# Column attention and a routed feed-forward on one core: low halves of v subtracted on GpSimd, and all of the last value pairs multiplied on halves

## The chip, the cores and the metric

One core of a Trainium2 chip runs the whole kernel. The metric is the device time of one execution in microseconds (us). A core has five engines that each work through an instruction stream of their own, in order, and wait for each other by semaphores: TensorE (PE in the profile, with PEld for the loading of its weights), VectorE (DVE), ScalarE (ACT), GpSimd (POOL) and SyncE (SP).

## The reference

`q`, `k` and `v` have the shape (4, 5056, 256). Attention runs over the columns, per batch, and its output rows go through eight experts, each of which takes exactly 2528 rows, given out greedily by the gate's value:

```python
qn = q / (np.linalg.norm(q, axis=1, keepdims=True) + 1e-06)
kn = k / (np.linalg.norm(k, axis=1, keepdims=True) + 1e-06)
a = softmax(kn.transpose(0, 2, 1) @ qn / tau)      # 256 x 256 per batch
x = (v @ a).reshape(B * S, D)                      # 20224 rows of 256
logits = x @ w_gate
# ... each expert e gets its cap = 2528 best rows, greedily over all (row, expert) values
out[mask] = np.maximum(x[mask] @ w1[e], 0.0) @ w2[e]
```

Everything is float32.

## The kernel before, in words

The kernel has three stages. In the first, some 200 us, the scores of the four batches are summed (L334) and the softmax is made; batch 0's product v @ a and the gate's logits are done beside it. In the second, from about 195 to 321 us, the rest of v @ a is multiplied, while the first expert's rows are searched out. In the third the eight experts' two layers run (L1333 and L1365), with the search for the next expert beside them.

The change is in the second stage, the loop over `later` near the program's end (L1406). `later` is a list of 52 **pairs** (b, c, t): two columns of 128 rows of v each, which `x_tiles` (L269) multiplies with the 256x256 matrix `a` of their batch into a PSUM tile `px`. There are two ways to do it:

- an **uncut** pair multiplies float32 by float32: 4 matmuls in the program (each shows as two records in the trace), from `vs` and `a_f`;
- a **cut** pair multiplies on halves: `split_v` (L255) makes a rounded high half `vh` on ACT (L259) and a low half `vl` = raw - `vh` (L262), and 12 matmuls of one pass sum `vh` x `aH`, `vh` x `aL` and `vl` x `aH`.

The set `cut` (L228, L229) says which pairs are cut. `cut_ahead` splits a pair AHEAD = 3 pairs before PE multiplies it; the tiles `vh` and `vl` have AHEAD + 1 = 4 buffers. ACT copies each `px` to `xs` (L286), and after two pairs starts a store of `xs` to `x_d` in HBM (L296).

Beside the pairs runs the **search** of the first expert (`route`, `search`, `totals`). It has two times four rounds and a last one. A round compares all keys with 15 thresholds on DVE (`ge`, L730, two instructions), counts on PE with 20 small matmuls (`pc` from `ge`, L699), reduces and spreads the counts on DVE (`Dm`, `Dr`, `Ex`: L702 to L708), sums over the partitions on PE with one matmul (`pc` from `Ex`, L712), and finds the new threshold on DVE (`mxs`, `hit`, `thr`, `cur`: L719 to L756). After the rounds a chain of small DVE instructions ends in the expert's number `ei` (L851) and in `cb` (L888). Then POOL loads the expert's weights (L1175), and `compact` turns the chosen rows into a list of indices with 20 matmuls `pi` (L912), whose rows ACT counts for 11 of them (`junk`, L930, and `ext`, L933). ACT and DVE split the loaded weights into halves in 8 pieces (L1184, L1187). When the pairs are stored and the list is there, POOL gathers the rows of the first chunk (L1225), PE turns them (L1291), ACT and DVE make `xH` and `xL` (L1300, L1303), and the first layer begins (L1333). Until the gathered rows have landed PE runs 27 dummy matmuls (`warm`, L1313).

The order of the instructions is fixed when the program is built. A planner, `Order`, keeps a clock for PE (`o.pe`) and one for DVE (`o.dve`). `tick` moves PE's clock on by each matmul, and `hook` then places every search step whose turn has come; DVE work that belongs to the pairs is handed over by `o.post` with a ready time and a cost:

```python
def post_low(low):
    unit[0] += 1
    o.post(o.pe + TURN_LAT, 690, low, unit[0])
```

The planner thus counts 690 ns of DVE for each `vl`. It keeps no clock for POOL.

Of the kernel before, what the change touches and what calls it, by code (L numbers as in the profile page):

```python
# [8 lines left out]
F32 = mybir.dt.float32  # L9
# [6 lines left out]
OP = mybir.AluOpType  # L16
# [32 lines left out]
CG = 128 // J  # L49
BUFS_V = 8  # L50
CUT_FROM = 12
CUT_TO = 40
GAP = 400
AHEAD = 3
AB = 2
# [36 lines left out]
def attention_moe(ctx: ExitStack, tc: tile.TileContext, q, k, vt, tau, wg, w1t, w2t, tabs, out):  # L92
    nc = tc.nc
    V = nc.vector
    S = nc.scalar
    P = nc.gpsimd
# [129 lines left out]

    later = [(b, c, t) for b, c in TODO for t in range(0, T, 2)]
    cut = {(0, c, t) for c in range(NCH) for t in range(0, T, 2)}  # L228
    cut |= set(later[CUT_FROM:CUT_TO] + later[CUT_TO::2])  # L229

    def is_cut(b, c, t):
        return (b, c, t - t % 2) in cut
# [9 lines left out]
    def cut_a(b, ac, post=None):  # L242
        aH = apool.tile([128, 2, GW], F32R, name="aH", bufs=AB)
        aL = apool.tile([128, 2, GW], F32R, name="aL", bufs=AB)
        S.activation(aH, ac, AF.Copy)
        a_cut[b] = (aH, aL)

        def low():
            V.tensor_tensor(aL, ac, aH.bitcast(F32), op=OP.subtract)
        if post:  # L250
            post(low)
        else:
            low()

    def split_v(b, c, t, post=None):  # L255
        raw = vs[b, c][:, :, t:t + 2, :]
        vh = vp.tile([128, 2, 2, 128], F32R, name="vh", bufs=AHEAD + 1)
        vl = vp.tile([128, 2, 2, 128], F32R, name="vl", bufs=AHEAD + 1)
        S.activation(vh, raw, AF.Copy)  # L259

        def low():
            V.tensor_tensor(vl, raw, vh.bitcast(F32), op=OP.subtract)  # L262
        if post:
            post(low)
        else:
            low()
        cuts_v[b, c, t] = (vh, vl)

    def x_tiles(b, c, t, xs, width, tick=None):  # L269
# [19 lines left out]
    def x_rows(width):  # L289
        xs = vp.tile([128, TH * GW], F32, name="xs", bufs=3)  # L290
        return xs[:, 0:TH * width].rearrange("p (t c) -> p t c", t=TH)

    def store_x(b, c, xs, t0, t1):
        r0 = (b * NCH + c) * CH
        rows = x_d[r0:r0 + CH].rearrange("(p t) c -> p t c", t=T)
        nc.scalar.dma_start(rows[:, t0:t1], xs[:, t0 % TH:t0 % TH + t1 - t0, 0:C])  # L296
# [738 lines left out]
    class Order:  # L1035
# [13 lines left out]
        def post(self, ready, cost, fn, unit):  # L1049
            self.main.append((ready, cost, fn, unit))  # L1050
# [76 lines left out]
    o = Order()  # L1127
    nphase = [0]

    def plan():  # L1130
        p = nphase[0]
        if p < E and done.get(("start", p)) is None and (p == 0 or done.get(("routed", p - 1))):
            done["start", p] = True

            def job(p=p):
                yield from route(p, E - p)
                done["routed", p] = True
                nphase[0] += 1
            o.add(job(), lambda p=p: 0 if (p == 0 or done.get(("idx", p - 1))) and (
                not done.get(("ei", p)) or done.get(("idx", p))) else EARLY_PRIO)  # L1140
# [21 lines left out]
    def settle():  # L1162
        for e in list(pend):
            if done.get(e[0]):
                pend.remove(e)
                e[1]()

    def want(key, fn):
        pend.append((key, fn))
        settle()  # L1170

    def load_w(p):
        raws[p] = big("ub"), big("ub")
        for raw, src in zip(raws[p], (w1t, w2t)):
            P.indirect_dma_start(out=raw, out_offset=None, in_=src,  # L1175
                                 in_offset=bass.IndirectOffsetOnAxis(ap=routed[p]["ei"][:, 0:1], axis=0))
# [58 lines left out]
    def gather():  # L1235
        for _ in range(2 if queue and queue[0][1] == 0 else 1):
            if queue:
                queue.pop(0)[2]()
# [4 lines left out]
    unit = [0]  # L1243
# [136 lines left out]
    with tc.manual_schedule():  # L1380
        o.dve = FIRST_LAT
        plan()
        cut_w = [None]

        def first_w():
            load_w(0)
            cut_w[0] = [o.pe + LOAD_LAT] + list(SPLIT)

        want(("ei", 0), first_w)
        o.patient = True  # L1390
        cutting = [st for st in later if st in cut]
        ready = {}

        def post_low(low):
            unit[0] += 1
            o.post(o.pe + TURN_LAT, 690, low, unit[0])

        def cut_ahead():
            st = cutting.pop(0)
            split_v(*st, post_low)  # L1400
            ready[st] = unit[0]

        for b in (2, 3):
            cut_a(b, a_f[b], post_low)

        for b, c, t in later:  # L1406
            if t % TH == 0:
                xs = x_rows(C)
            due = later.index((b, c, t)) + AHEAD
            while cutting and later.index(cutting[0]) <= due:  # L1410
                cut_ahead()
            o.flush(max((ready.get(st, 0) for st in later[:due + 2 - AHEAD]), default=0))
            x_tiles(b, c, t, xs, C, o.tick)
            settle()
            if cut_w[0] and o.pe > cut_w[0][0] and len(cut_w[0]) > 1:
                split_piece(0, *cut_w[0].pop(1))
            if (b, c) == TODO[-1] and t >= TH:
                store_x(b, c, xs, t, t + 2)
            elif t % TH == TH - 2:
                store_x(b, c, xs, t + 2 - TH, t + 2)  # L1420
        o.until(("ei", 0))
        settle()
        o.until(("idx", 0))
        actx.close()
        cctx.close()
        ffx = ctx.enter_context(tc.tile_pool(name="ffx", bufs=2))
        ps_1 = ctx.enter_context(tc.tile_pool(name="ps_1", bufs=DEPTH, space=PSUM))
        ps_2 = ctx.enter_context(tc.tile_pool(name="ps_2", bufs=2, space=PSUM))
        o.margin = FIRST_MARGIN
        o.patient = False  # L1430
        load_x(0, 0)
        while queue:
            gather()
        load_x(0, 1, paced=True)
        for i, q_, eng in cut_w[0][1:]:
            split_piece(0, i, q_, eng)
        for _ in range(START_TICKS):
            warm()
            o.tick(216 + 80)
        turn(0, 0)  # L1440
        for p in range(E):
            last = p == E - 1
            if p == 1:
                o.margin = MARGIN
            def turn_at(c):
                return lambda: turn(p, c)

            turns = [] if last else [(p + 1, 0), (p + 1, 1)]

            def next_turn(force=False):  # L1450
                if not turns:
                    return
                if force:
                    o.until(("idx", p + 1))
                    settle()
                    while queue:
                        gather()
                    while o.pe < landed[turns[0]]:
                        o.tick(100)
                if o.pe >= landed.get(turns[0], 1e12):  # L1460
                    turn(*turns.pop(0))

            def next_w(p=p):
                if p + 1 < E:
                    want(("ei", p + 1), lambda: load_w(p + 1))

            nchunk = len(cuts[p])
            h = {}
            pieces = {} if p == 0 else {at: [lambda q_=q_: split_piece(p, 1, q_, None)] for q_, at in enumerate((1, 3, 4, 6))}
            if p == 0:  # L1470
                next_w()
                h[0] = layer1(p, 0, {}, 2)
                layer2(p, 0, h[0], {1: [turn_at(1)]})
                h[1] = layer1(p, 1, {5: [turn_at(2)]})
            else:
                if (p, 1) not in xts:
                    fb = 5 if (p, 1) in BY_PE else TURN_FB
                    pieces[fb] = pieces.get(fb, []) + [turn_at(1)]
                h[0] = layer1(p, 0, pieces, 2)
                next_w()  # L1480
            for c in range(1 if p else 2, nchunk):
                h[c] = layer1(p, c, {}, 2 if p else 1)
                ins = {}
                if c + 1 < nchunk:
                    ins = {min(1, cuts[p][c - 1] - 1): [turn_at(c + 1)]}
                elif not last:
                    def w1(p=p):
                        o.until(("ei", p + 1))
                        settle()
                        g = split_w(p + 1, 0, V)  # L1490
                        for _ in g:
                            o.dve += 600
                    ins = {min(1, cuts[p][c - 1] - 1): [w1]}
                layer2(p, c - 1, h[c - 1], ins)
            layer2(p, nchunk - 1, h[nchunk - 1], {i: [next_turn] for i in range(1, 4)})
            while turns and turns[0][1] == 0:
                next_turn(True)
# [63 lines left out]
```

## Time and profile before

| | |
|---|---|
| median of 3 runs | 1256.83 us (1256.02 to 1259.64) |
| the profiled execution | 1257.59 us, of which 1255.8 us span |
| PE busy | 1238.3 us (99%) |
| DVE busy | 872.7 us (69%) |
| ACT busy | 601.0 us (48%) |
| POOL busy | 384.5 us (31%) |
| granted TensorE clock, mean | 0.998 |

The span reaches from the first to the last instruction. Busy time counts overlapped matmuls with their latency, so PE can be 99% busy and still stand still for short times; the spacing of the matmuls' starts shows more. The profile lets one ask for any stretch, engine, line or tile. The chain of waits follows the work that ended last backwards from the end.

### The profile page before, as it was taken

The page shows a single profiled execution, that of the slowest core. Times are in us where ns is not written, and L with a number is a line of the kernel's source. Part 1 is how long each engine was busy: PE and PEld are TensorE (multiplying, and loading weights), DVE is VectorE, ACT ScalarE, POOL GpSimd, SP SyncE. Part 2 cuts the span into 40 slices and gives each one's busy share as a digit, 9 for nine tenths or more (in the row PEclk, how much of TensorE's full clock was granted, in tenths as well). Part 3 has the DMA queues.
Part 4 walks back from the last instruction along what each step waited for, and adds up shares of the span by engine and source line. Part 5 has one row for each costly group of instructions (what it writes and reads, how often), then busy time and mean ns, then how long its engine had stood idle before and what let it go on. Part 6 is the DMA issues. An engine that isn't in the chain of part 4 may idle for free.

```text
span 1255.8 us, 24082 instructions
## 1 busy us (share of the span) xinstructions
PE 1238.3 (99%) x8779; PEld 1111.2 (88%) x8779; DVE 872.7 (69%) x2457; ACT 601.0 (48%) x1441; POOL 384.5 (31%) x690
## 2 busy tenths in 40 slices
PE   8999999999999999999999999999999999999998
PEld 6888977898888988998999899988989898898998
DVE  6688496898778778868867888887785445344431
ACT  6646652467324434434533755556554554334331
POOL 1000010000432353244343452532444434334322
PEclk9999999999999999999999999999999999999999
DMA  8999875236112134143422532341434235333301
GB/s 308 314 409 414 311 275 199 118 153 235 58 48 87 41 84 121 42 90 81 126 68 59 138 79 64 80 131 40 93 73 129 59 80 146 73 69 76 69 31 34
DMA packets 184759, 160.33 MB, mean 128 GB/s; under 512 B 150080, under 2 KB 155328, under 8 KB 180032
## 3 DMA queue, kind: packets, MB, share of 16 engines
q1 hardware_dynamic: 157712, 79.33, 22.6%
q0 software_dynamic: 17664, 58.22, 14.4%
q10 hardware_dynamic: 9264, 21.24, 4.4%
q8 instruction: 69, 1.13, 0.4%
q14 instruction: 50, 0.41, 0.1%
HBM read 99.97 MB, written 41.68 MB: 113 GB/s over the span
## 4 chain that ended last, share of the span: by engine, by line
PE 84%; DVE 6%; issue 5%; POOL 2%; DMA 2%; ACT 1%; SPq 0%; POOLq 0%; DVEq 0%; ACTq 0%
PE ph L1333 33%; PE py L1365 32%; PE px L283 7%; PE s L334 7%; PE pc L699 2%; POOL out_dram L1372 1%; PE px L446 1%; DVE acc_q L348 1%; PE pi L912 1%; DVE yy L405 1%; DVE acc_k L348 1%; DMA x_d<-xs 1%; DMA ua<-in_q_dram 1%; DVE vl L262 0%; ACT ua L1184 0%
## 5 line engine op out<-in xcount | busy, mean ns | idle before, releaser
L1333 PE MATMUL ph<-xH,ua 128*128 128x512 f32 (+3 forms) x1312 | 354.8, 388 | 0.3 <-ACT xH L1300 0.3
L1365 PE MATMUL py<-uc,hH 128*128 128x256 f32 (+1 forms) x2560 | 334.5, 279 | 0.0
L1341 DVE SCALAR_TENSOR_TENSOR hL<-ph,hH 128x512 fp32r<-128x512 f32 (+3 forms) x328 | 219.4, 670 | 162.4 <-ACT hH L1336 158.2
L1365 PEld LDWEIGHTS py<-uc,hH 128*128 128x128 f32 (+1 forms) x2560 | 312.9, 187 | 2.2
L1372 POOL DMA_INDIRECT out_dram<-y,idx x160 | 162.0, 1013 | 498.1 <-ACT y L1370 445.3
L1336 ACT ACTIVATE hH<-ph 128x512 fp32r<-128x512 f32 (+3 forms) x328 | 190.6, 582 | 206.1 <-PE ph L1333 202.1
L1333 PEld LDWEIGHTS ph<-xH,ua 128*128 128x128 f32 x1312 | 238.4, 189 | 42.8 <-ACT xH L1300 0.4
L1333 PE MATMUL ph<-xL,ua 128*128 128x512 f32 (+3 forms) x656 | 201.3, 386 | 0.1
L1370 ACT ACTIVATE y<-py 128x256 f32<-128x256 f32 (+1 forms) x160 | 61.3, 383 | 251.0 <-PE py L1365 235.1
L1225 POOL DMA_INDIRECT xg<-x_d,src x156 | 156.6, 1004 | 71.6 <-issue 33.6
L1365 PE MATMUL py<-uc,hL 128*128 128x256 f32 (+1 forms) x1280 | 178.3, 280 | 0.0
L1365 PEld LDWEIGHTS py<-uc,hL 128*128 128x128 f32 (+1 forms) x1280 | 160.2, 187 | 0.0
L1333 PEld LDWEIGHTS ph<-xL,ua 128*128 128x128 f32 x656 | 122.1, 189 | 23.3 <-DVE xL L1303 0.3
L334 PE MATMUL s<-ua 128*128 128x256 f32 x320 | 73.7, 387 | 2.6 <-DMA ua<-in_q_dram 2.6
L334 PEld LDWEIGHTS s<-ua 128*128 128x128 f32 x320 | 61.0, 193 | 14.2 <-issue 3.4
L286 ACT ACTIVATE xs<-px 128x512 f32<-128x512 f32 (+1 forms) x96 | 49.4, 528 | 49.5 <-PE px L283 47.8
L334 PE MATMUL s<-uc 128*128 128x256 f32 x320 | 71.3, 380 | 0.0
L334 PEld LDWEIGHTS s<-uc 128*128 128x128 f32 x320 | 60.3, 190 | 8.8 <-issue 0.8
L283 PE MATMUL px<-aH,vh 128*128 128x256 f32 (+1 forms) x216 | 62.7, 292 | 0.0
L283 PE MATMUL px<-aH,vl 128*128 128x256 f32 (+1 forms) x216 | 61.3, 284 | 1.1 <-DVE vl L262 0.9
L1284 DVE TENSOR_TENSOR xL<-ph,xH 128x512 fp32r<-128x512 f32 (+1 forms) x66 | 42.9, 679 | 27.8 <-ACT xH L1281 25.7
L969 ACT ACTIVATE junk<-pi,rhalf 128x160 bf16<-128x160 f32 x140 | 54.0, 391 | 15.7 <-PE pi L912 14.6
(341 smaller groups left out, 1569.5 us busy)
## 6 DMA issues: line engine op xcount, KB each, us to landing
x_d<-xs ACTq DMA_DIRECT2D x39, 512.0 KB
xq<-xg SPq DMA_DIRECT2D x500, 32.0 KB
vr<-in_vt_dram SPq DMA_DIRECT2D x14, 1024.0 KB
uc<-in_k_dram SPq DMA_DIRECT2D x18, 512.0 KB
uc<-in_q_dram SPq DMA_DIRECT2D x18, 512.0 KB
ua<-in_k_dram SPq DMA_DIRECT2D x17, 512.0 KB
ua<-in_q_dram SPq DMA_DIRECT2D x17, 512.0 KB
out_dram<-y,idx POOLq DMA_INDIRECT x160, 2.4
```

The source lines that it names most:

```text
L283: mm = PE.matmul(px[:, i * C:i * C + width], lhsT=l_, rhs=a_, start=(j == 0), stop=(j == len(terms) - 1))
L286: S.activation(xs[:, t % TH:t % TH + n, 0:width], px[:, 0:n * width].rearrange("p (t c) -> p t c", t=n), AF.Copy)
L334: newest[0] = PE.matmul(sb[:, ib * C:(ib + 1) * C], lhsT=kt[:, t, ib * 128:(ib + 1) * 128], rhs=qt[:, t, :], start=(first and t == 0 and i ...
L969: S.activation(junk, pi[:, i * W:i * W + COLS], AF.Sign, bias=rhalf[:, g0 + i:g0 + i + 1], scale=-1.0, accum_out=sgn[:, g0 + i:g0 + i + 1])
L1225: P.indirect_dma_start(out=xg[:n, i, :], out_offset=None, in_=x_d, in_offset=bass.IndirectOffsetOnAxis(ap=at, axis=0))
L1284: V.tensor_tensor(xL[:, kb, 0:nt], pt[:, 0:nt], xH[:, kb, 0:nt].bitcast(F32), op=OP.subtract)
L1333: PE.matmul(ph[:, 0:nt], lhsT=l[:, w], rhs=x_[:, kb, 0:nt], start=(i == 0), stop=(i == 5))
L1336: S.activation(hH[:, fb, 0:nt], ph[:, 0:nt], AF.Relu)
L1341: V.scalar_tensor_tensor(hL[:, fb, 0:nt], ph[:, 0:nt], 0.0, hH[:, fb, 0:nt].bitcast(F32), op0=OP.max, op1=OP.subtract)
L1365: PE.matmul(py[:n, 0:C], lhsT=l[:, fb, tk], rhs=w[:, d], start=(j == 0), stop=(j == 23))
L1370: S.activation(y[:n], py[:n, 0:C], AF.Copy)
L1372: sd = P.indirect_dma_start(out=out, out_offset=bass.IndirectOffsetOnAxis(ap=idx[:n, col:col + 1], axis=0), in_=y[:n], in_offset=None)
```

## The change

Four things are edited:

- `split_v` no longer posts the subtraction to the planner. It issues it at once on an engine that it is given. In the loop over `later` that engine is GpSimd (P). Batch 0's pairs, and those of `halves`, keep VectorE.
- `cut` now takes all pairs of `later` from the thirteenth on: 40 in place of 34. The six added ones are every second of the last twelve.
- The `flush` before each pair, which had placed the DVE subtractions due by then, now only places the two subtractions for `aL` of batches 2 and 3 (L249), ahead of the first pair.
- The planner's DVE clock no longer moves for a `vl`.

```diff
     cut = {(0, c, t) for c in range(NCH) for t in range(0, T, 2)}
-    cut |= set(later[CUT_FROM:CUT_TO] + later[CUT_TO::2])
+    cut |= set(later[CUT_FROM:])
...
-    def split_v(b, c, t, post=None):
+    def split_v(b, c, t, eng=V):
         raw = vs[b, c][:, :, t:t + 2, :]
...
         S.activation(vh, raw, AF.Copy)
-
-        def low():
-            V.tensor_tensor(vl, raw, vh.bitcast(F32), op=OP.subtract)
-        if post:
-            post(low)
-        else:
-            low()
+        eng.tensor_tensor(vl, raw, vh.bitcast(F32), op=OP.subtract)
         cuts_v[b, c, t] = (vh, vl)
...
         def cut_ahead():
-            st = cutting.pop(0)
-            split_v(*st, post_low)
-            ready[st] = unit[0]
+            split_v(*cutting.pop(0), P)
...
         for b in (2, 3):
             cut_a(b, a_f[b], post_low)
+        lows_a = unit[0]
...
-            o.flush(max((ready.get(st, 0) for st in later[:due + 2 - AHEAD]), default=0))
+            o.flush(lows_a)
```

The lines of the changed program lie 1 to 9 lower (L262 becomes L260, L283 becomes L277, L699 becomes L693, and so on).

The first place where the order moves is DVE, in one round of the search (here the third; before):

```order
L730 TENSOR_TENSOR ge<-hi,thr 128x10x120 x2
L741 TENSOR_SCALAR pre<-steps,cur 128x15
L262 TENSOR_TENSOR vl<-ua,vh 128x512 x2
L702 TENSOR_TENSOR Dm<-pc,dmask 128x64
L705 TENSOR_REDUCE Dr<-Dm 128x8
L708 TENSOR_TENSOR Ex<-Dr,jsel 120x128
L262 TENSOR_TENSOR vl<-ua,vh 128x512
L719 TENSOR_REDUCE mxs<-pc 128x15
```

The same round on DVE in the changed program:

```order
L724 TENSOR_TENSOR ge<-hi,thr 128x10x120 x2
L735 TENSOR_SCALAR pre<-steps,cur 128x15
L696 TENSOR_TENSOR Dm<-pc,dmask 128x64
L699 TENSOR_REDUCE Dr<-Dm 128x8
L702 TENSOR_TENSOR Ex<-Dr,jsel 120x128
L713 TENSOR_REDUCE mxs<-pc 128x15
```

The three subtractions have left the round. On PE, the matmuls of cut pairs that stand between the last of the 20 counting matmuls and the summing one are 10 now, where they were 12; between the summing one and the next 20 they are mostly 25 now, where they were 17 to 36. Up to the matmul on `cb` (L894) PE has 304 matmuls of cut pairs, where it had 343, and 176 after it.

The second place is POOL, in the whole second stage, before and in the changed program:

```order
L1024 MEMSET ge 128x2560
L1175 DMA ub<-in_w1t_dram,ei 128x2048
L1175 DMA ub<-in_w2t_dram,ei 128x2048
L1224 MEMSET spacer 1x1
L1225 DMA xg<-x_d,src 128x256
```

```order
L1018 MEMSET ge 128x2560
L260 TENSOR_TENSOR vl<-ua,vh 128x512 x8
L260 TENSOR_TENSOR vl<-uc,vh 128x512 x8
L260 TENSOR_TENSOR vl<-vr,vh 128x512 x12
L1169 DMA ub<-in_w1t_dram,ei 128x2048
L1169 DMA ub<-in_w2t_dram,ei 128x2048
L260 TENSOR_TENSOR vl<-vr,vh 128x512 x12
L1218 MEMSET spacer 1x1
L1219 DMA xg<-x_d,src 128x256
```

POOL now has 40 subtractions, 28 ahead of the weight loads and 12 behind them.

The third place is ACT, from about the first counted `junk` on, before and in the changed program:

```order
L296 DMA x_d<-xs 128x1024
L930 ACTIVATE junk,sgn<-pi,rhalf 128x160 x2
L286 ACTIVATE xs<-px 128x512
L259 ACTIVATE vh<-vr 128x512
L930 ACTIVATE junk,sgn<-pi,rhalf 128x160
L933 ACTIVATE ext<-pi 128x6
L286 ACTIVATE xs<-px 128x512
L296 DMA x_d<-xs 128x1024
```

```order
L258 ACTIVATE vh<-vr 128x512
L924 ACTIVATE junk,sgn<-pi,rhalf 128x160
L280 ACTIVATE xs<-px 128x512
L258 ACTIVATE vh<-vr 128x512
L924 ACTIVATE junk,sgn<-pi,rhalf 128x160
L280 ACTIVATE xs<-px 128x512
L290 DMA x_d<-xs 128x1024
L258 ACTIVATE vh<-vr 128x512
L924 ACTIVATE junk,sgn<-pi,rhalf 128x160
L927 ACTIVATE ext<-pi 128x6
```

From the first `junk` to the last `xs` ACT has 14 `xs`, 10 `vh`, 11 `junk`, 4 `ext`, 8 weight pieces and 6 stores in the changed program; before, it has 10 `xs`, 3 `vh`, 11 `junk`, 4 `ext`, 7 weight pieces and 5 stores.

## Rows read from the trace of the kernel before

**Rows 1.** Busy time of each engine in two stretches of the second stage.

```profile
core 0: us, PE busy (x) PEld busy (x) DVE busy (x) ACT busy (x) POOL busy (x), PEclk, DMA share, GB/s
...
245.00:260.00 15.00, 15.00 (x173) 14.87 (x172) 14.24 (x38) 10.27 (x19) 0.00 (x0) 1.00 0.41 163
...
300.00:312.00 12.00, 11.06 (x68) 9.81 (x67) 10.93 (x35) 11.27 (x32) 0.00 (x0) 1.00 0.54 218
```

**Rows 2.** Chain of waits in order of time: start us, us, what.

```profile
222.04 14.01 PE px L283 x64
...
254.23 4.30 PE px L283 x36
...
321.85 7.23 PE ph L1333 x44
```

**Rows 3.** Timeline, end of the stage: start us, us, engine, line, operation.

```profile
312.19 0.33 ACTq L296 DMA_DIRECT2D x_d<-xs  x1
...
316.08 0.95 POOL L1225 DMA_INDIRECT xg<-x_d,src  x1 [23.50 <-DVE eq L602]
```

**Rows 4.** Groups of DVE by shape: busy us, mean ns | idle before.

```profile
L262 DVE TENSOR_TENSOR vl<-vr,vh 128x512 fp32r<-128x512 f32 x38 | 25.3, 684 | 1.8 <-ACT vh L259 1.7
```

**Rows 5.** Timeline of DVE in one round of the search.

```profile
249.11 0.28 DVE L719 TENSOR_REDUCE mxs<-pc 128x15 f32<-128x120 f32 x1
...
249.64 0.28 DVE L749 SCALAR_TENSOR_TENSOR thr<-n_hit,pre 128x120 int16<-128x120 f32 x1
...
249.96 1.48 DVE L730 TENSOR_TENSOR ge<-hi,thr 128x1200 bf16<-128x1200 int16 x2
251.35 1.29 DVE L262 TENSOR_TENSOR vl<-ua,vh 128x512 fp32r<-128x512 f32 x2
...
253.29 0.29 DVE L708 TENSOR_TENSOR Ex<-Dr,jsel 120x128 fp32r<-120x128 f32 x1
```

**Rows 6.** Timeline of PE: the same round, and the list's first matmuls.

```profile
248.85 0.22 PE L712 MATMUL pc<-Ex,ones_q 128*128 128x128 f32 x1
...
251.91 0.76 PE L699 MATMUL pc<-eq,ge 128*128 128x64 bf16 x20
...
254.00 0.22 PE L712 MATMUL pc<-Ex,ones_q 128*128 128x128 f32 x1
...
290.88 0.18 PE L894 MATMUL pc<-cb,before 128*128 128x1 bf16 x1
...
292.92 0.58 PE L912 MATMUL pi<-E__106,G 128*128 128x162 bf16 x6
```

**Rows 7.** Timeline of ACT, last part of the stage.

```profile
295.01 0.39 ACT L930 ACTIVATE junk<-pi,rhalf 128x160 bf16<-128x160 f32 x1 [0.40 <-ACT xs L286]
...
303.56 0.60 ACT L286 ACTIVATE xs<-px 128x512 f32<-128x512 f32 x1
304.05 0.62 ACT L1184 ACTIVATE ua<-ub 128x512 fp32r<-128x512 f32 x1
304.57 0.62 ACT L259 ACTIVATE vh<-vr 128x512 fp32r<-128x512 f32 x1
305.10 0.38 ACT L930 ACTIVATE junk<-pi,rhalf 128x160 bf16<-128x160 f32 x1
```

**Rows 8.** Timeline of POOL, then of DVE, in the first stage.

```profile
50.78 1.27 POOL L372 TENSOR_TENSOR ny<-ny,nd 128x4 f32<-128x4 f32 x1
...
156.87 1.08 POOL L368 TENSOR_SCALAR ny<-ny 128x4 f32<-128x4 f32 x1 [37.73 <-ACT ny L367]
...
196.04 0.20 POOL L372 TENSOR_TENSOR ny<-ny,nd 128x4 f32<-128x4 f32 x1
...
50.76 1.23 DVE L348 TENSOR_TENSOR acc_q<-acc_q,sq 128x1024 f32<-128x1024 f32 x1 [0.35 <-ACT acc_q L344]
...
156.65 1.23 DVE L348 TENSOR_TENSOR acc_k<-acc_k,sq 128x1024 f32<-128x1024 f32 x1 [0.48 <-ACT acc_k L344]
```

**Rows 9.** Groups and timeline of POOL: its two nearest larger instructions.

```profile
L136 POOL IOTA rgrid<- 128x2560 int16 x1 | 2.3, 2257 | 0.0
...
29.77 0.52 POOL L327 MEMSET ua<- 64x512 f32 x1 [25.96 <-DMA ua<-in_k_dram]
```

More of the change, by code (lines that the diff above doesn't have):

```diff
@@ L51 @@
 CUT_FROM = 12
-CUT_TO = 40
 GAP = 400
@@ L1391, in attention_moe @@
         cutting = [st for st in later if st in cut]
-        ready = {}
         def post_low(low):
```

## The prediction

> **What bounds the kernel now.** I read the stretches first, then the chain of waits, then the timelines of single engines. From 245 to 260 us PE is busy for 15.00 of 15.00 us and DVE for 14.24, at full clock; from 300 to 312 ACT leads with 11.27 of 12 and PE has gaps [rows 1]. So the second stage has two halves: up to the end of the search PE is full and DVE nearly so, and behind it ACT sets the pace. The reader should see that POOL does nothing there: 0.00 in both.
>
> The stage ends in a fixed chain. The last store of x is issued at 312.19, the first gather goes out at 316.08 [rows 3], and the first layer starts at 321.85 [rows 2]. The gather must wait for that store, so whatever moves the last pair moves all that follows; the third stage is PE work of unchanged amount. I forecast the shift of the last store and take it over one to one.
>
> **The price of a pair on PE.** Uncut matmuls run 64 records in 14.01 us, 0.219 us each; a pair has 8 records, 1.75 us. Cut ones run 36 in 4.30, 0.119 each; a pair has 12, 1.43 us [rows 2]. Six pairs change over: 6 x 0.32 = 1.9 us less PE work. They lie in the half where ACT sets the pace, so I do not book this; it is in the second rival.
>
> **What leaves DVE.** 34 subtractions of 684 ns (38 of this shape stand in the row with others of batch 0 and (1, 0); those from other tiles take the same) [rows 4], three of them in the round shown; in all 34 x 0.684 = 23 us. The planner moves the search forward: PE reaches the matmul on `cb` 39 matmuls earlier, 39 x 0.119 = 4.6 us. By the plan that matmul, at 290.88 [rows 6], would come at 286.3.
>
> The two subtractions for `aL` now stand ahead of the search. The first count is put four uncut matmuls later, 1.75 us on PE; pairs fill that place, so it costs nothing by itself, and it is inside the 4.6 us.
>
> **The half behind the search.** From the first `junk` ACT works without a stop. Spacings of starts: `xs` 0.49, a weight piece 0.52, `vh` 0.53, `junk` 0.38; a store leaves ACT idle for 0.40 behind an `xs` and costs some 0.5 [rows 7]. Before: 10 x 0.49 + 3 x 0.53 + 7 x 0.52 + 11 x 0.38 + 5 x 0.5 + 0.4 for the small copies = 17.2 us. Measured, from 295.01 [rows 7] to the last store's issue at 312.19 [rows 3]: 17.2. After: 14 x 0.49 + 10 x 0.53 + 8 x 0.52 + 11 x 0.38 + 6 x 0.5 + 0.4 = 23.9. The first `pi` comes 2.0 us behind `cb` (290.88 to 292.92) [rows 6] and a `junk` some 0.4 later: 286.3 + 2.4 + 23.9 = 312.6, against 312.19. **Without any collision the change gives nothing: +0.4 us.** The 4.6 us are given back on ACT, which has seven more `vh` and four more `xs` behind that point.
>
> **What POOL takes over.** No row shows a POOL subtraction of this size. The nearest: filling 512 elements takes 0.52 us, writing 2560 takes 2.257, that is 0.45 for 512 [rows 9], and the smallest two-input instruction 0.20 [rows 8]. If its two reads come one after the other, 0.20 + 2 x 0.45 = 1.1 us, my estimate; lower end 0.52, upper end three passes, 0.20 + 3 x 0.45 = 1.55. At 1.1 POOL alone keeps up with PE's 1.43 per pair. At 1.55 it would not quite, but three pairs of lead cover it.
>
> **The collision.** An addition of 4 elements takes POOL 0.20 us when DVE is quiet, and 1.27 when DVE has just begun a sum of two SBUF tiles: begun at 50.78, ended at 52.05, DVE's sum ran from 50.76 to 51.99. A one-input instruction was held the same way, from 156.87 to 157.95, with DVE's sum ending at 157.88 [rows 8]. So POOL stands still for the whole of a two-input DVE instruction. The rows do not show whether DVE stands still for a long POOL instruction: none of POOL's reads here is long. I take it to hold both ways, since nothing in the rows makes DVE the preferred one.
>
> [...]
>
> Now one round. PE's places, in the changed order: 25 matmuls from the summing matmul to the counting ones, 3.0 us; 20 counting ones and 10 more, 0.6 + 1.2; in all 4.8 us with 35/12 = 2.9 pairs. DVE without collisions needs, behind the summing matmul at 248.85, until 251.44 (249.96 + 1.48), 2.6 us; and from the counting start at 251.91 to `Ex` done at 253.58, 1.7 us [rows 5, 6]. Slack: 0.4 + 0.1 = 0.5 us a round. The planner has closed up exactly the room that `vl` had filled, and it knows nothing of POOL.
>
> [...] PE is in order, so a late DVE step stops the pairs too.
>
> Eight rounds lie beside cut pairs: 8 x 0.8 = 6.4 us. Between the last count and `cb` stand some ten more two-input instructions of 0.3 to 0.5 us; two or three held up by half of 1.1: 1.2 us. Sum 7.6, and the 0.4: **+8.0 us**. The profiled execution has 1257.59, so it would have 1265.6; it lies 0.76 above the median of 1256.83, and shifted from the median the time is 1264.8 us. [...]
>
> The weight loads stand behind 28 subtractions and wait for `ei`; PE is at pair 25 there, so the subtraction behind them is not due for two pairs, and they cost nothing.
>
> **Rivals.** *First, POOL alone gives way*. [...] For it: every held instruction in the rows is POOL's. Against it: no row tests the other way. It turns into the forecast's side where DVE is held for more than 0.5 us a round.
>
> *Second, ACT finds its room*: its `junk` and `vh` fit beside PE, and PE sets the end. From 286.3, 176 matmuls x 0.119 = 20.9, and 20 `pi` at some 0.075, 1.5: 308.7 for the last matmul, where the last one was about 311.6. That is -2.9, 1253.9 us. For it: `vh` runs three pairs ahead. Against it: 11.27 of 12 busy [rows 1], and no collision must occur.
>
> [...]
>
> **Chances.** 0.3% of the time, 3.8 us, is about what a measurement of this kernel can tell from no change. The forecast, with ends from +3.8 to +12: 0.42. The third rival: 0.13. The first, with what lies between it and +3.8: 0.30. The second: 0.15, of which 0.07 lie beyond -3.8, where both the collision and ACT's limit would have to be wrong. Slower 0.55, same 0.38, faster 0.07. The range takes in the second rival and the third: 1253.5 to 1272; the forecast's own is 1260.6 to 1268.8.
>
> **What would show it.** Right: `vl` on POOL at 1.1 us where free and longer beside `ge`; `ge`, `thr` or `Ex` on DVE longer than 0.78, 0.28 and 0.29; PE idle ahead of the counting or summing matmul, released by DVE; the last store at about 320. Wrong: DVE's durations unchanged and PE without gaps up to `cb`, with the last store at 312 or before. The ACT step is wrong if ACT has idle time behind the first `junk` and the store still comes before 311.

## Result, and the profile after

The changed kernel takes **1276.24 us** (1271.63 to 1279.38, 4 runs), the kernel before beside it 1257.48: a ratio of 1.0145, with a 95% interval of [1.0119, 1.0171]. On another chip the same pair gave 1274.10 against 1257.55, 1.0137 [1.0120, 1.0155]. The forecast was 8.0 us; the loss is 16.6 to 18.8 us. The sign was right, the time lies outside the range.

The profiled execution after took 1276.17 us, of which 1274.4 us span. Busy time of each engine, the same stretches as [rows 1] and one more:

```profile
core 0: us, PE busy (x) PEld busy (x) DVE busy (x) ACT busy (x) POOL busy (x), PEclk, DMA share, GB/s
245.00:260.00 15.00, 14.00 (x147) 12.98 (x147) 12.82 (x27) 8.68 (x15) 10.06 (x8) 1.00 0.35 141
260.00:275.00 15.00, 12.76 (x133) 12.07 (x132) 12.63 (x28) 8.13 (x15) 11.19 (x8) 1.00 0.35 140
300.00:312.00 12.00, 9.34 (x76) 8.83 (x76) 11.40 (x37) 6.52 (x19) 9.16 (x8) 0.93 0.74 261
```

PE, full before, now has gaps during the search, and at 300 us the search is only just ending; from 300 to 312 us DVE, not ACT, is the busiest. What PE waited for between 240 and 302 us (engine and line, releaser: us in total, times, longest):

```profile
PE pc L693 <- DVE ge L724: 2.8, 4, 1.3
PE pc L706 <- DVE Ex L702: 2.4, 3, 0.8
PE pc L888 <- DVE cb L882: 1.3, 1, 1.3
PE pc L816 <- DVE tb L813: 0.9, 1, 0.9
PE pc L693 <- DVE ge L773: 0.5, 1, 0.5
```

Always DVE. For `vl` from POOL, PE hardly waits (0.8 us in all up to the last pair). The subtractions on POOL, against [rows 4] on DVE, by shape:

```profile
L260 POOL TENSOR_TENSOR vl<-vr,vh 128x512 fp32r<-128x512 f32 x24 | 33.5, 1404 | 16.1 <-ACT vh L258 14.6 <-ACT ext L927 1.5
...
L260 POOL TENSOR_TENSOR vl<-uc,vh 128x512 fp32r<-128x512 f32 x8 | 11.8, 1491 | 3.8 <-ACT vh L258 3.8
```

And the timeline of a round as it ran, on DVE (to be held against [rows 5]), then on POOL:

```profile
262.08 3.61 DVE L724 TENSOR_TENSOR ge<-low,th 128x1200 bf16<-128x1200 int16 x2
...
268.10 0.28 DVE L743 SCALAR_TENSOR_TENSOR thr<-n_hit,first 128x120 int16<-128x120 f32 x1
...
268.42 2.44 DVE L724 TENSOR_TENSOR ge<-low,thr 128x1200 bf16<-128x1200 int16 x2
270.79 1.24 DVE L735 TENSOR_SCALAR pre<-steps,cur 128x15 f32<-128x15 f32 x1
271.95 0.21 DVE L696 TENSOR_TENSOR Dm<-pc,dmask 128x64 f32<-128x64 f32 x1
```

```profile
262.00 4.84 POOL L260 TENSOR_TENSOR vl<-uc,vh 128x512 fp32r<-128x512 f32 x3 [0.85 <-ACT vh L258]
268.24 1.29 POOL L260 TENSOR_TENSOR vl<-uc,vh 128x512 fp32r<-128x512 f32 x1 [1.40 <-ACT vh L258]
270.28 2.95 POOL L260 TENSOR_TENSOR vl<-uc,vh 128x512 fp32r<-128x512 f32 x2 [0.76 <-ACT vh L258]
```

POOL begins three subtractions in a row at 262.00, DVE its two comparisons at 262.08. The comparisons take 3.61 us in place of 1.48, the three subtractions 4.84 in place of about 3 x 1.29: as if the two engines took turns here, since one after the other they would need 1.48 + 3.87 = 5.3 us. `pre`, 15 elements, takes 1.24 us beside a subtraction. `Dm`, beside one too, takes 0.21 us, before 0.22 to 0.23.

The timeline of the end of the stage, engines mixed, for [rows 3] and the last of [rows 2] and [rows 6]:

```profile
300.44 0.16 PE L888 MATMUL pc<-cb,before 128*128 128x1 bf16 x1 [1.27 <-DVE cb L882]
...
330.31 0.33 ACTq L290 DMA_DIRECT2D x_d<-xs  x1
...
335.81 1.06 POOL L1219 DMA_INDIRECT xg<-x_d,src  x1 [7.62 <-issue]
...
341.31 1.07 PE L1327 MATMUL ph<-xH,ua 128*128 128x256 f32 x3 [0.22 <-ACT xH L1294]
```

`cb` is 9.6 us later than before, the last store 18.1 (330.31 - 312.19), the first layer 20.4 (its first matmul was at 320.89 before; the 321.85 of [rows 2] is only where the chain of waits enters that layer). From there to the end it is 933.1 us, before 934.9: none of the loss lies in the third stage.

### The profile page after: what moved, and what is told of

It is laid out like the page before. It is cut to its first block, busy times and chain, and to the rows that moved or that the text cites. A ratio compares the mean times of both kernels' runs of the same rounds, so it can differ in the third digit from the quotient of the medians.

```text
span 1274.4 us, 24159 instructions
## 1 busy us (share of the span) xinstructions
PE 1244.7 (98%) x8803; PEld 1115.9 (88%) x8803; DVE 880.4 (69%) x2423; ACT 602.8 (47%) x1447; POOL 437.4 (34%) x730
## 3 DMA queue, kind: packets, MB, share of 16 engines
q0 software_dynamic: 17664, 58.22, 14.2%
## 4 chain that ended last, share of the span: by engine, by line
PE 81%; DVE 10%; issue 5%; POOL 2%; ACT 1%; DMA 1%; POOLq 0%; SPq 0%; DVEq 0%; ACTq 0%
PE ph L1327 31%; PE py L1359 30%; PE s L328 8%; PE px L277 6%; PE pc L693 2%; PE px L440 1%; DVE ge L724 1%; POOL out_dram L1366 1%; DVE acc_q L342 1%; PE pi L906 1%; DVE acc_k L342 1%; DVE ua L1181 1%; DVE yy L399 1%; DMA ua<-in_q_dram 0%; PE ph L1285 0%
## 5 line engine op out<-in xcount | busy, mean ns | idle before, releaser
L277 PE MATMUL px<-aH,vl 128*128 128x256 f32 (+1 forms) x240 | 69.1, 288 | 1.2 <-DVE vl L260 0.9
L277 PE MATMUL px<-aH,vh 128*128 128x256 f32 (+1 forms) x240 | 69.3, 291 | 0.0
L277 PE MATMUL px<-aL,vh 128*128 128x256 f32 (+1 forms) x240 | 68.8, 287 | 0.0
L963 ACT ACTIVATE junk<-pi,rhalf 128x160 bf16<-128x160 f32 x140 | 54.0, 391 | 16.2 <-PE pi L906 13.8
```

The source lines that it names most:

```text
L277: mm = PE.matmul(px[:, i * C:i * C + width], lhsT=l_, rhs=a_, start=(j == 0), stop=(j == len(terms) - 1))
L963: S.activation(junk, pi[:, i * W:i * W + COLS], AF.Sign, bias=rhalf[:, g0 + i:g0 + i + 1], scale=-1.0, accum_out=sgn[:, g0 + i:g0 + i + 1])
```

## The experiments

The runs are cut at the same four events of their trace: the first counting matmul, the matmul on `cb`, the last matmul on `px`, the first matmul of the first layer (us between them; "old" is the plan of the kernel before with DVE time counted for each `vl`, "closed" the changed plan):

| run | low halves on | plan, pairs | count to `cb` | `cb` to last `px` | to first layer | to the end |
|---|---|---|---|---|---|---|
| before | DVE | old, 34 | 55.0 | 20.3 | 9.8 | 934.9 |
| e9_fill_old_order | POOL, fill | old, 34 | 54.7 | 21.5 | 9.7 | 979.9 |
| e8_engine_only | POOL | old, 34 | 64.6 | 19.9 | 9.7 | 933.8 |
| e11_closed_dve | DVE | closed, 34 | 65.3 | 30.1 | 11.6 | 933.3 |
| e1_pool_34 | POOL | closed, 34 | 58.7 | 26.6 | 9.9 | 970.0 |
| e16_pool_34_again | POOL | closed, 34 | 59.3 | 26.6 | 10.0 | 933.5 |
| e2_six_dve | DVE | old, 40 | 55.0 | 20.5 | 12.4 | 978.6 |
| e7_old_plan | POOL | old, 40 | 64.5 | 20.7 | 12.3 | 981.1 |
| after | POOL | closed, 40 | 58.7 | 28.9 | 11.9 | 933.1 |
| e12_as_changed | POOL | closed, 40 | 58.8 | 27.9 | 12.0 | 932.5 |
| e10_aL_late | POOL | closed, 40, `aL` late | 60.4 | 29.7 | 12.0 | 935.1 |
| e3_fill_once | POOL, fill | closed, 40 | 48.4 | 25.0 | 13.5 | 933.8 |
| e4_fill_thrice | POOL, 3 fills | closed, 40 | 48.4 | 25.4 | 13.5 | 972.8 |

The 979.9, 970.0 and 972.8 are from a chip with pauses, below. Ratios are against the kernel before on the same chip. Two theories stood at first: **hold**, the 'lock' of the recorded expectations (DVE and POOL hold each other up while POOL subtracts, as forecast, only dearer) and **order** (the closed-up plan itself loses, whoever subtracts), and beside them POOL's **rate**.

**The engine alone, order word for word as before** (`e8_engine_only`):

```diff
+            P.tensor_tensor(vl, raw, vh.bitcast(F32), op=OP.subtract)
+            post(lambda: None)
-            post(low)
```

> Before's order word for word, 34 pairs cut, with the low halves subtracted on GpSimd; the planner still leaves room for them on VectorE. Theory 'lock': VectorE's search steps still meet GpSimd's reads, 1.3 us each, but there are 0.7 us of room for each subtraction that left; +4 to +12 us against before, with ge, thr, Ex and pre long on VectorE. Theory 'order': 0. Theory 'slow GpSimd' (1.3 us a subtraction, TensorE waits for vl): 1.3 is below the 1.43 us of a pair, 0 to +2 us, with TensorE waits on vl.

1266.86 us, 1.0070 [1.0053, 1.0087]. Nothing but the engine differs, and `cb` comes 9.6 us later behind the first count; the rest is as long as before. PE's waits between 236 and 303 us are DVE's again:

```profile
PE pc L700 <- DVE ge L731: 3.7, 4, 1.3
PE pc L823 <- DVE tb L820: 1.8, 1, 1.8
PE pc L713 <- DVE Ex L709: 1.5, 3, 0.6
```

**The same order, zeros written in place of the subtraction** (`e9_fill_old_order`; the low halves of 34 pairs are left out of the sum):

```diff
-            P.tensor_tensor(vl, raw, vh.bitcast(F32), op=OP.subtract)
+            P.memset(vl.bitcast(F32), 0.0)
```

> The kernel before with its order of work kept on every engine but VectorE and GpSimd; GpSimd fills the low halves of the 34 pairs with zeros (0.54 us each in the run that filled once) and VectorE's 34 subtractions are gone. The subtractions themselves are left out. If what the change loses is VectorE and GpSimd holding each other up while GpSimd subtracts: 1254 to 1259 us, no slower than the kernel before, and the search's comparison stays at 0.78 us, pre at 0.23 us. If it is GpSimd's signalling, its place in the chain, or any work on it at all: near the run that subtracted on GpSimd in the same order, 1264 to 1268 us. A gain of more than 4 us (below 1253) would say that VectorE's time for the low halves was on the path.

0.9996 [0.9975, 1.0017]. This chip takes 1299.77 us for the kernel before, with pauses of all engines in the third stage (979.9 us in this run). Whole times from it do not carry over: the closed plan with 34 pairs gives 1.0041 there and 1.0113 on another chip (`e1_pool_34` and `e16_pool_34_again`, below), while its second stage is the same on both to 0.6 us. So the argument goes by the second stage. POOL has work in the same places and `cb` is not late: 54.7 against 55.0 us (behind it, 21.5 against 20.3). So it is the subtraction that costs 9.6 us, and taking 34 x 0.684 us from DVE gains nothing by itself.

**The changed kernel with one fill, and with three** (`e3_fill_once` with `range(1)`, `e4_fill_thrice` with `range(3)`, as here; the low halves of 40 pairs are left out of the sum):

```diff
-        eng.tensor_tensor(vl, raw, vh.bitcast(F32), op=OP.subtract)
+        if eng is P:
+            for _ in range(3):
+                P.memset(vl.bitcast(F32), 0.0)
+        else:
+            eng.tensor_tensor(vl, raw, vh.bitcast(F32), op=OP.subtract)
```

> The change's order word for word, but in place of each of the 40 subtractions GpSimd fills vl with zeros (the low halves of these pairs are left out of the sum): 0.52 us that write SBUF and read nothing. Theory 'lock': VectorE's steps are back at their lengths of before and the order runs as planned, -3 to +2 us against before. Theory 'order': the loss stays, +15 us or more. Theory 'slow GpSimd': gone as well, 0.

> The changed kernel with GpSimd writing zeros three times over each low half in place of the subtraction: about 1.6 us of GpSimd per pair (three times the 0.54 us of one fill), more than the subtraction's 1.3 us, but with no two operands read. The subtractions of these 40 pairs are left out. If the loss is GpSimd's rate (pairs come ready too late): 1270 us or more, as the changed kernel's 1276, with TensorE waiting for vl. If the loss is the two engines holding each other up: 1261 to 1268 us, near the 1264 of a single fill, and the comparison stays at 0.78 us.

1.0049 [1.0033, 1.0064] and 1.0061 [1.0039, 1.0082]. With three fills POOL works 3 x 0.534 = 1.6 us per pair, longer than a subtraction (1.26 to 1.30 us where free), and the count-to-`cb` time is 48.4 us in both: rate is out. Yet the first ratio is a loss of 6.2 us, above the expected -3 to +2 and above the forecast's +0.4 without a collision. In the run with three, the group of POOL's fills from 230 to 330 us (busy us, mean ns), and the second view, DVE's comparisons of one kind (ns min/median/max):

```profile
L262 POOL MEMSET vl<- 128x512 f32 x108 | 56.1, 534 | 25.6 <-PE px L281 21.1
```

```profile
L728 DVE TENSOR_TENSOR ge<-low,thr x6: 774/780/784, 263.9 to 274.5; 128x1200 bf16<-128x1200 int16 x6
```

None of the six is longer than 0.784 us beside fills; beside subtractions, in the changed kernel, the longest takes 1.88. One-operand instructions are another matter. With three fills, `pre` and `low`, 0.23 and 0.24 us beside one fill, become

```profile
265.30 1.07 DVE L739 TENSOR_SCALAR pre<-steps,cur 128x15 f32<-128x15 f32 x1
...
258.90 0.77 DVE L768 TENSOR_SCALAR low<-w 128x160 int16<-128x160 f32 x1
```

while POOL only writes. Ten DVE instructions up to `cb`, most of them with one operand, are longer than beside one fill, and none of it reaches `cb` (48.4 in both). The closed plan with fills in place of the subtractions thus brings `cb` 6.6 us nearer to the first count, but the run still loses 0.5 to 0.6%: nearly 5 us come back behind `cb`, 3.7 in the last step, and the first count itself is 4.4 us later (240.3 against 235.9).

**Six more pairs on DVE, and on POOL, by the old planner** (`e2_six_dve`: the kernel before with the first edit; `e7_old_plan`: the changed kernel, POOL subtracting, with the second, and `ready` and the `flush` as before):

```diff
-    cut |= set(later[CUT_FROM:CUT_TO] + later[CUT_TO::2])
+    cut |= set(later[CUT_FROM:])
```

```diff
-            split_v(*cutting.pop(0), P)
+            st = cutting.pop(0)
+            split_v(*st, P)
+            post_low(lambda: None)
+            ready[st] = unit[0]
```

> The six more pairs cut, and all low halves left on VectorE. Theory 'lock' (VectorE stands still while GpSimd reads SBUF for a subtraction): no GpSimd read is added, so nothing of the loss is here; six pairs are 1.9 us less TensorE work in a stretch where ScalarE sets the pace, -2 to +1 us against before. Theory 'six pairs' (the added cut pairs with their ScalarE and TensorE work are what costs): +5 us or more. Theory 'order' (the order that the planner wrote without the subtractions costs, not the engine): about 0.

> As the change (40 pairs cut, on GpSimd), but the planner goes on counting 690 ns of VectorE for each subtraction, so that TensorE reaches the search's matmuls where it did before. Theory 'lock': the closed-up order was a part of the loss; less than the change's +18.8 us, by the 0.5 to 1 us of room in each of eight rounds: +8 to +14 us against before. Theory 'order': 0, all of the loss gone.

1305.26 us, 1.0378 [1.0361, 1.0395], and 1316.34, 1.0469 [1.0451, 1.0486]: both far off what was expected. The second stage does what it should: 55.0 and 64.5 us to `cb`, the hold of 9.6 once more. But this plan also moves the third stage: there PE of `e2_six_dve` waits for gathered rows,

```profile
PE ph L1333 <- DVE xL L1284: 16.0, 3, 6.2
PE ph L1333 <- ACT xH L1281: 9.2, 2, 8.2
```

which come through SP's queue; at 1045 to 1085 us PE is busy for 24.94 of 40. Both have the same plan and lose 44 and 46 us there, so it is the plan, not the engine. Why it places the gathers so late was not followed up. The closed plan does not do this.

**The fourth case of engine and order** (`e11_closed_dve`) and the third (`e1_pool_34`, repeated as `e16_pool_34_again`); `e1` is the changed kernel with the old set of 34 pairs, `e11` also has V for P:

```diff
-    cut |= set(later[CUT_FROM:])
+    cut |= set(later[CUT_FROM:40] + later[40::2])
...
-            split_v(*cutting.pop(0), P)
+            split_v(*cutting.pop(0), V)
```

> 34 pairs and the closed-up order of work, as in the run with 34 pairs on GpSimd, but the 34 subtractions on VectorE: the fourth of four cases of engine and order. It has 2.9 subtractions of 0.69 us, 2.0 us, in a round that the planner closed up to about 4.8 us with 0.5 us to spare. If VectorE's own time is then the limit: 1.5 us late a round, eight rounds, 60 to 62 us from the first count to cb against 48.4 without any subtraction, and a ratio of 1.003 to 1.012, as bad as GpSimd. If the closed-up order suits VectorE too: 48 to 53 us there, and a ratio of 0.997 to 1.002.

> The changed kernel with 34 pairs cut as before the change, all 34 low halves on GpSimd, and the closed-up order of work. If the hold of the two engines is the loss and the six more pairs are worth what they save on TensorE (six times 0.32 us, beside ScalarE's pace): 1270 to 1278 us, as the changed kernel. If the six more pairs cost much of it (six more subtractions that meet VectorE): 1262 to 1269 us. If the closed-up order costs nothing, as the run with the old order on GpSimd: near its 1266.9 us.

> The changed kernel with 34 pairs cut as before, closed-up order, all on GpSimd, as once on the second chip (where it was 1.0041, with pauses of all engines in the third stage that the first chip does not show). On a chip like the first: by that run's trace 96 us from the first counting matmul to the first layer, where the changed kernel has 99.6 and 98.7; so a ratio 0.002 to 0.004 below the changed kernel's, 1.009 to 1.012. If the six more pairs cost nothing: 1.0135 to 1.0145.

`e11`: 1281.89 us, 1.0191 [1.0177, 1.0205], worse than expected and worse than POOL: 65.3 us to `cb`. The closed plan has no room for the subtractions on DVE. `e1`: 1.0041 [1.0021, 1.0060] on the chip with pauses, where its second stage is as the closed plan's with POOL (58.7 and 26.6 us). `e16`: 1271.10, 1.0113 [1.0098, 1.0129], so 0.0024 to 0.0032 below the changed kernel's two ratios; the six more pairs cost some 3 us (the intervals touch, but the traces say the same): 26.6 against 27.9 and 28.9, 10.0 against 11.9 and 12.0. The last step shows where two of them go. With 34 pairs the last two stores are issued 1.7 us apart (2.9 in `e16`) and the gather follows 3.9 us behind the last ([rows 3]: 312.19 and 316.08; 3.6 in `e16`). With all of the last pairs cut they are 1.0 apart and the gather follows after 5.5 (after: 329.31, 330.31, 335.81; `e3_fill_once`: 5.5 too, where the last store took 4.40 us to land, against 2.42 in `e8_engine_only`). In most runs, then, the stores give back what PE saves on the last pairs. They are not the whole of it: in `e10_aL_late`, below, the last stores are 1.0 us apart too, the gather follows after 3.6, and the last step takes 12.0 all the same. There PE, in order, has the next expert's first counts and sums ahead of the gathered rows and turns these only at 339.11, 6.7 us behind the gather. In the changed kernel PE also waits 2.81 us for such a count (`ge`) just ahead of them. How the 2.2 us divide between the two was not tried.

**The moved subtractions for `aL`** (`e10_aL_late`) beside the changed kernel itself (`e12_as_changed`):

```diff
-            o.flush(lows_a)
+            o.flush(lows_a if later.index((b, c, t)) >= CUT_FROM - 1 else 0)
```

> The changed kernel itself, as the mark for the other three on the same chip: a ratio of 1.010 to 1.017 to the kernel before, as on the first chip (1.0145). Its second stage, from the traces: 58 to 59 us from the first counting matmul to the matmul on cb, 28 to 29 us from there to the last pair, 11.5 to 12.5 us from there to the first layer.

> The changed kernel with the two subtractions for aL put back to where they stood before the change, behind the first comparison of the search. If their new place, in the middle of the last batch's softmax on VectorE, holds TensorE up: the last uncut pair of batch 1 ends 1 to 2.5 us earlier in its profile and the time falls by 1 to 3 us against the changed kernel. If pairs fill that place, as the prediction had it: within 1 us of the changed kernel.

1274.10 and 1276.15 us: putting them back gains nothing. In the changed plan one stands in the last softmax on DVE, a transpose has moved ahead of the softmax's end, and `ac` starts 11.75 us behind ACT's last copy of `ac` (201.09 to 212.84 in the profile after) where it took 10.42 before and takes 10.43 with the two put back. The first count comes 1.7 us later behind the last pair of column chunk (1, 1); put back, the two take DVE's time in the search, 60.4 us to `cb` in place of 58.8.

**Does the hold of `pre` cost time?** (`e6_pre_sum` in all searches, `e13_pre_sum_first` in the first alone, `e14_pre_sum_64` with a wider tile, `e15_tile_only` with the tile alone):

```diff
-    V.tensor_scalar(pre, steps[:, i + 1], cur, None, op0=OP.add)
+    V.tensor_scalar(pre, steps[:, i + 1], cur, 0.0, op0=OP.add, op1=OP.add, accum_out=rtile("pre_n", (128, 1)))
```

In `e13` and `e14` this stands under `if p == 0`; in `e14` the tile is `rtile("pre_n", (128, 16))`, of which the first column is used; `e15` leaves the instruction alone:

```diff
                         pre = rtile("pre", (128, NT))
+                        if p == 0:
+                            rtile("pre_n", (128, 1))
```

> The changed kernel with one instruction of each search round (pre, a 15-element TENSOR_SCALAR that grew from 0.23 to 1.25 us in three of four) written with a running sum beside it. If the one-operand form is held because of how it reads, and the form with a sum is not: pre at 0.25 to 0.35 us in all four, and 1271 to 1277 us, since pre lies ahead of the first comparison of a round only in part. If any VectorE instruction is held while GpSimd subtracts: pre still above 1 us in two or three of four, and 1275 to 1279 us.

> The changed kernel with pre written with a running sum in the first expert's search only; the later searches keep the plain form. The run with it in all searches gave a ratio of 1.0316 on the second chip, most of it in the third stage. If that came from the sums in the later searches: this one gives the changed kernel's ratio or up to 0.003 less, and the third stage is as long as the changed kernel's. If the sum in the first search did it: a ratio near 1.03 again. If hold-ups of pre matter for the end of the search: 1 to 2 us less from the first count to cb than the changed kernel; the earlier run's 58.7 us, the same as the changed kernel's, speaks against that.

> The run with the running sum in the first search alone, but with the tile that takes the sum 64 bytes wide per partition in place of 4, so that every tile of the kernel behind it starts at a multiple of 64 bytes again if it did before. If the 4 bytes, which shift other tiles, made the third stage 19 us longer (matmuls of the second layer every 0.1198 us in place of 0.1173): back at 0.117 and at the changed kernel's ratio, 1.011 to 1.017. If the instructions of the sum did it: 0.1198 again and a ratio of 1.026 to 1.031.

> The changed kernel with the tile of 4 bytes per partition set aside and never used; every instruction as in the changed kernel. If the shift of the other tiles made the third stage longer: a ratio of 1.026 to 1.031 and 0.1198 us between matmuls of the second layer. If the instructions of the sum did it: 1.011 to 1.017 and 0.117.

`e6` 1.0316 [1.0288, 1.0344], `e13` 1.0288 [1.0265, 1.0311], `e14` 1.0281 [1.0263, 1.0300], `e15` 1.0292 [1.0272, 1.0312]. The form with a sum takes 0.22 us; the changed kernel first, then `e6` (ns min/median/max), both in the first search:

```profile
L735 DVE TENSOR_SCALAR pre<-steps,cur x4: 221/1247/1252, 246.1 to 278.0; 128x15 f32<-128x15 f32 x4
```

```profile
L735 DVE TENSOR_SCALAR_CACHE_REDUCE pre<-steps,cur x4: 215/216/220, 243.1 to 275.0; 128x15 f32<-128x15 f32 x4
```

The plain form takes 1.25 us in three of four, the form with a sum 0.22 in all four. Yet 58.7 us to `cb` stay 58.7: where `pre` takes 0.22 us, `Ex` behind it takes 1.38 in place of 0.87 (both in the third round). The loss of these four has another cause: `e15`, which has each instruction of the changed kernel and only sets a 4-byte tile per partition aside, loses as much, and 64 bytes do not mend it. In all four the second layer's matmuls stand further apart. The chain of waits, the changed kernel, then `e15`:

```profile
811.32 4.45 PE py L1359 x38
```

```profile
816.80 4.61 PE py L1361 x38
```

0.117 against 0.121 us each; the mean spacing over the whole stage is 0.1168 against 0.1199, and 0.1199 to 0.1207 in the other three. Over the whole stage, the second layer's matmuls (ns min/median/max), after and in `e15`:

```profile
L1359 PE MATMUL py<-uc,hH x2560: 276/276/385, 348.6 to 1269.6; 128*128 128x256 f32 x187, 128*96 128x256 f32 x10
```

```profile
L1361 PE MATMUL py<-uc,hH x2560: 276/280/386, 346.9 to 1285.9; 128*128 128x256 f32 x187, 128*96 128x256 f32 x10
```

The third stage takes 950.6 us, after 933.1. So setting this tile aside changes PE's pace, 0.1168 to 0.1199 us; by what was not shown. Against `e15`, which has the same pace, `e13` and `e14` differ by 0.0004 and 0.0011, within their intervals: the hold of `pre` costs nothing that can be measured.

No run beat the kernel before.

## Why the prediction was wrong

**What bounds the kernel**: right. PE and DVE set the first half, ACT the second, and all moves the third stage along, which is 1.9 to 2.5 us shorter than before.

**The plan's 4.6 us, and the half behind the search**: right, and shown by the fills. With one fill, the first count comes 1.7 us later behind the last pair of chunk (1, 1) (8.9 against 7.1 us, `e3_fill_once`) and `cb` 6.6 earlier behind the count, -4.9 together; behind `cb` 25.0 us in place of 20.3, +4.7. The forecast had -4.6 and +5.0. But "without any collision the change gives nothing: +0.4" did not follow: that run is 6.2 us slower, since its last step is 3.7 us longer and its first stage, with the clock spoken of below, some 2.7.

**POOL's 1.1 us**: too low, 1.26 to 1.30 where free, inside its bounds.

**The hold goes both ways**: right (`e8_engine_only` against `e9_fill_old_order`). The first rival, POOL alone giving way, is refuted: the comparison grew from 0.78 to 1.88 us. The second rival, ACT finding its room, is refuted too: it had the last matmul 22.4 us behind `cb`, and even with fills it comes after 25.0. The third, DVE and POOL taking turns, is nearest with 1272.0 us, the upper end of the range, but by luck: its price is an estimate that no run shows. The rounds lost 7.9 us, and behind `cb`, where it had nothing, 2.9 and 3.9 more were lost. Something like such turns shows in the rows at 262.00 and 262.08.

**The step that failed** is the price of the collision, in three terms of the sum. *The hold up to `cb`* was mis-sized: 0.8 a round and "two or three held up by half of 1.1", in all 7.6 us. No run shows the 0.8, an estimate of the author's; eight rounds lost 7.9 us, 1.0 each. Measured: 58.75 - 48.38 = 10.4 us (in the old plan with 34 pairs 64.6 - 55.0 = 9.6), of which 7.9 lie between the first and the ninth count, forecast 6.4, and 2.5 between there and `cb`, forecast 1.2.

Held against the run with one fill instruction by instruction, 21 of DVE's 116 instructions from the first comparison to `cb` are longer by more than 0.1 us, 18.9 us together. In the rounds 16 are held and lose 0.90 us on average, most often 1.0 to 1.1. Of these 14.4 us only 7.9 reach the end, 0.8 a round being lost in slack, where the forecast had 0.5. In the chain behind the last count five are held (`tie`, `mk`, `jk`, `pb`, `ei`), 4.5 us. The forecast looked at two-input instructions only and left out one-operand forms, `pre` (0.23 to 1.25 us) and `mk` (0.29 to 1.32), though by the runs with a sum `pre` did not matter.

*The hold was taken to end at `cb`*: behind it nothing was booked. There 12 subtractions meet DVE's list work: 27.9 and 28.9 us against 25.0 with one fill, 2.9 and 3.9 us, the largest error of the three. The worst place, in the timelines before and after: `asg`, 0.33 us, then 3.30 beside three subtractions. Here POOL did not take turns; its three ran on at 1.3 us each while `asg` stood through what was left of all three:

```profile
294.95 0.33 DVE L868 TENSOR_TENSOR asg<-asg,t 128x160 f32<-128x160 f32 x1
```

```profile
303.48 3.78 POOL L260 TENSOR_TENSOR vl<-vr,vh 128x512 fp32r<-128x512 f32 x3
...
304.15 3.30 DVE L862 TENSOR_TENSOR asg<-asg,t 128x160 f32<-128x160 f32 x1
```

*The last step* was moved along unchanged at 9.8 us, and the six more pairs, "I do not book this", were taken as free. It takes 11.9 and 12.0 us, 2.2 more, by the stores and the order on PE above.

The two profiled executions of the changed kernel are 18.6 and 13.8 us slower than the profile before. The forecast 8.0, the missing 2.8, 3.9 and 2.9, and 2.2 make 16.9 and 15.9. The first stage adds 4.0 and 0.8: the last matmul of chunk (1, 1) starts at 232.8 and, in `e12_as_changed`, at 229.6, before at 228.8. The third stage takes off 1.9 and 2.5. Together that is 19.0 and 14.2, within 0.5 of both. The 4.0 go with the clock: from 215 to 226 us the mean granted clock is 0.70 in the profile after, behind two waits of PE of 1.60 and 0.69 us; in `e12_as_changed`, with the same two waits, it is 1.00, as it is before, where they are 0.3 and 0.7 us. Such a dip shows in 8 of the 12 profiles with the closed plan (0.69 to 0.84) and in 2 of the 5 with the old one (0.84, 0.85); whether the change makes it deeper or more frequent is not shown.

## What to carry to other kernels

An idle engine is not a free engine: before moving work to GpSimd, list for the stretch in question which VectorE instructions would meet it, one-operand forms too, and book each meeting at most of the GpSimd instruction's length (here 0.9 of 1.28 us) and more where GpSimd has several queued (3.0 us once), up to the end of the chain and not only to its first landmark. Change the engine alone in the old order, and put a fill in its place, before changing the plan: these two runs gave the price of the hold in that order, 9.6 us, and showed that VectorE's freed 23 us were worth nothing. A gain on the last piece before a fixed chain has to be followed through that chain, here into the stores and the next search's first counts.

## Not expected of the hardware

- A 15-element instruction with one SBUF operand takes 1.25 us beside a GpSimd subtraction, as if it were a large one; with a running sum written beside it, 0.22.
- GpSimd's fills, 0.534 us each and up to 1.6 us a pair, leave VectorE's comparisons at 0.78 us, but three of them in a row hold a 15-element `tensor_scalar` for up to 0.85 us.
- A tile of 4 bytes per partition that nothing uses made the third stage 17 us longer, with the same instructions in the same order: 276 ns median of a second-layer matmul became 280, and they stand further apart by 2.6% (0.1168 to 0.1199 us). The cause is open.
- One of the chips ran the kernel before in 1299.77 us, all others in 1257; the ratio of another kernel to it was 1.0041 there and 1.0113 elsewhere.
